# Adding two partial sums by accumulating transfers: an attention and MLP kernel on one Trainium2 core

## The chip, the core and the metric

The kernel runs on one core of one Trainium2 chip. A core has TensorE (matrix products, PE in the profile, with its weight loads as PEld), VectorE (DVE), ScalarE (ACT), GpSimd (POOL) and SyncE (SP). Each runs its own list of instructions in order, and they wait for each other by semaphores. Transfers (DMA) are issued by SP, ACT or POOL from their own lists, and a transfer issued by one of them is behind everything that stands earlier in that engine's list. The metric is the time of one execution on the device in microseconds. Three runs of the kernel before gave 1382.28, 1385.5 and 1387.74 us, so its median is 1385.5 us.

## The reference

The input x has 2048 tokens of 640 values. It is normalised once; xn goes through an attention block with 32 heads of 20 values, and through an MLP block with its own normalisation, 1536 hidden values and GELU. The output is x + attention + MLP.

```python
def _A_ref(x, wqkv, wo):
    ...
    scores = jnp.einsum("bhqd,bhkd->bhqk", q, k) * (Dh ** -0.5)
    p = _softmax(scores, axis=-1)
    o = jnp.einsum("bhqk,bhkd->bhqd", p, v)
    return (lambda x, *d: x.transpose(*d))(o, 0, 2, 1, 3).reshape(B, S, D) @ wo

def _B_ref(x, w1, b1, w2, b2):
    y = _layernorm(x, axis=-1)
    h = _gelu(jnp.einsum("bsd,df->bsf", y, w1) + b1)
    return jnp.einsum("bsf,fd->bsd", h, w2) + b2

x = A_x
xn = _layernorm(x, axis=-1)
return x + _A_ref(xn, A_wqkv, A_wo) + _B_ref(xn, B_w1, B_b1, B_w2, B_b2)
```

## The kernel before

The kernel has three stages. Up to about 290 us it normalises x, projects it to q, k and v, and splits the MLP's weights into two 16-bit halves. From there to about 1310 us it runs attention, with the MLP's products filled in between. After that comes the last part of the output projection.

**Attention.** Heads go in pairs `g`, tokens (queries) in two halves `hf` of 1024. The order of the 32 pieces is fixed in `ORDER`. A piece has two column halves `cc` of 512 queries, and 16 key blocks `kb` each. For every key block `scores` issues two products into the PSUM tile `s` (line 584) and one exponential on ScalarE into `p` (L586). For half of the key blocks (`SPLIT`) VectorE takes the lower half of p, `low` (L598), which `rest` records. `pv` issues the products with the values (L615) for a group of four key blocks, one group later than its scores. So TensorE needs a `low` about one group after VectorE could have made it.

Because of how the values lie in the array, each head's result comes in two partial sums. The products go to 32-row strips of the PSUM tile `o`; strips 0 and 1 belong to the first head of a pair, 2 and 3 to the second, and the two strips of one head have to be added. The same holds for the row sums, the softmax's denominators, which are a column of ones in the value matrix. `unload` writes the strips from the tile `ev` to scratch memory in HBM: `opart[p]` for the values and `lpart[p]` for the row sums, with p = 0 and 1 for the two partial sums.

**Finishing.** When a set of 2 or 3 pairs (`UNITS`, so 4 or 6 heads) is complete for one half of the tokens, `finish` loads the partial sums again, now as [heads x 20 rows, 512 tokens], and makes the normalised result. There are 12 finishes. Eleven have two chunks of 512 tokens (`w = 512`), the last one (`last`) has one of 1024. Per finish, the row sums are loaded to the tile `lt` (L675), added (L702), checked and inverted (L704 to L707), written to `linv` (L709) and read back spread over 20 rows per head as `rb` (L721). Per chunk, the two halves are loaded to the tile `oa` (L697), added (L725), multiplied by rb (L727), split into two 16-bit halves (L729, L731) and written to `oscr` (L732). The tile `oa` has one buffer, and the split result lies in the second half of it, so the loads of the second chunk wait for the write to oscr of the first.

**What sets the order.** The order of instructions is written out by hand: `finish` is a generator, and `tick` takes one step of each generator in `sides` after every two key blocks. Each `yield` in `finish` therefore moves what follows two key blocks later in the list of every engine. The loop takes MLP products from `fill` by a credit count, which does not depend on the generators in `sides` before the projection. MLP products go through one PSUM buffer (`psM`): VectorE must read it (L740 for the first layer, L757 for the second) before TensorE may start the next.

**Transfers.** Nearly all are issued by SP. GpSimd issues one kind in the attention stretch: `load_xb` loads 128 rows of x to the tile `xb` from SP (L808), and then GpSimd adds the bias b2 onto it by an accumulating transfer (L809). This occurs sixteen times.

Of the kernel before, what the change touches and what calls it, by code (L numbers as in the profile page):

```python
# [12 lines left out]
ALU = mybir.AluOpType  # L13
# [29 lines left out]
def mha_mlp_kernel(tc, x, wqkv, wo, w1, b1, w2, b2, out):  # L43
    nc = tc.nc
# [3 lines left out]
    with (  # L48
# [12 lines left out]
        opart = dram.tile([2, D, S], F32, name="opart")  # L61
        lpart = dram.tile([2, 2, H, S // 2], F32, name="lpart")
# [449 lines left out]
        with ExitStack() as scope:  # L512
# [127 lines left out]
            def dma(g, hf):  # L640

                return (nc.scalar if (g, hf) == ORDER[-1] else nc.sync).dma_start

            def unload(g, hf, ev):
                cols = slice(hf * 1024, (hf + 1) * 1024)
                for p in range(2):
                    dma(g, hf)(lpart[p, hf, 2 * g : 2 * g + 2, :].rearrange("a (c t) -> a c t", c=2),
                                      ev[PAD + DH + VW * p :: 64])
                    for a in range(2):
                        q0, r = 64 * a + PAD + VW * p, (2 * g + a) * DH  # L650
                        dma(g, hf)(opart[p, r : r + DH, cols].rearrange("d (c t) -> d c t", c=2),
                                          ev[q0 : q0 + DH])
                if g + 1 in ENDS:
                    fins.append(finish(g + 1 - UNITS[ENDS.index(g + 1)], g + 1, hf))
                    if len(fins) == 1:
                        sides.append(finishing())
# [9 lines left out]
            def finish(g0, g1, hf):  # L666
                nh, r0, r1 = 2 * (g1 - g0), 2 * g0 * DH, 2 * g1 * DH
                last = (g1 - 1, hf) == ORDER[-1]
                go = dma(g1 - 1, hf)
                w = 1024 if last else 512  # L670
                lt = m1.tile([P, 2, 64], F32, tag="lt", name="lt")
                n = checks.pop()
                yield
                for p in range(2):
                    go(lt[: nh * 16, p, :], lpart[p, hf, 2 * g0 : 2 * g1, :].rearrange("h (b t) -> (h b) t", t=64))  # L675
                for c0 in range(0, 1024, w):
                    cols = slice(hf * 1024 + c0, hf * 1024 + c0 + w)
                    if last:
                        o0, o1 = (ptp.tile([P, 2, 512], F32, tag="p", name="oa").rearrange("p c t -> p (c t)")
                                  for _ in range(2))  # L680
                        rb = o0

                        sel = [ptp.tile([P, 2, 512], F32, tag="p", name="sel").rearrange("p c t -> p (c t)")
                               for _ in range(2)]
                        for b0, t in zip((0, 8), sel):
                            nc.gpsimd.tensor_copy(
                                t[: nh * 16, : 8 * nh * DH].rearrange("p (b h d) -> p b h d", b=8, h=nh),
                                ident[: nh * 16, : nh * 16].rearrange("p (h b) -> p b h", b=16)[:, b0 : b0 + 8, :, None]
                                .to_broadcast([nh * 16, 8, nh, DH]))
                    else:  # L690
                        o = m1.tile([P, 2, 512], F32, tag="oa", name="oa")
                        o0, o1 = o[:, 0], o[:, 1]
                        rb = m1.tile([P, 512], F32, tag="rb", name="rb")
                    hl = o1.bitcast(F16).rearrange("p (s t) -> p s t", s=2)[: r1 - r0]
                    o0, o1, rb = o0[: r1 - r0], o1[: r1 - r0], rb[: r1 - r0]
                    for p, o in enumerate((o0, o1)):
                        go(o, opart[p, r0:r1, cols])  # L697
                    if c0 == 0:
                        for _ in range(W1 if last else 4):
                            yield  # L700
                        l = lt[: nh * 16]
                        nc.vector.tensor_add(l[:, 0], l[:, 0], l[:, 1])  # L702

                        nc.vector.tensor_scalar(l[:, 1], l[:, 0], LO, None, ALU.is_ge, ALU.min,  # L704
                                                accum_out=good[: nh * 16, n : n + 1])
                        nc.vector.tensor_scalar(l[:, 0], l[:, 0], 1e-30, None, ALU.max)
                        nc.vector.reciprocal(l[:, 1], l[:, 0])  # L707
                        if not last:
                            go(linv[hf, 2 * g0 : 2 * g1, :].rearrange("h (b t) -> (h b) t", t=64), l[:, 1])  # L709
                        for _ in range(4 if last else 1):  # L710
                            yield
                    if last:

                        rb = psS.tile([P, 2, 512], F32, tag="s", name="rb")[: nh * DH]
                        for b in range(16):
                            nc.tensor.matmul(rb[:, b // 8, b % 8 * 64 : b % 8 * 64 + 64],
                                             sel[b // 8][: nh * 16, b % 8 * nh * DH : (b % 8 + 1) * nh * DH],
                                             l[:, 1], start=True, stop=True)
                        rb = rb.rearrange("p c t -> p (c t)")
                    for h in range(0 if last else nh):  # L720
                        go(rb[h * DH : (h + 1) * DH],  # L721
                           linv[hf, 2 * g0 + h : 2 * g0 + h + 1, c0 : c0 + w].to_broadcast([DH, w]))
                    for _ in range(W2 if last else 4):
                        yield
                    nc.vector.tensor_add(o0, o0, o1)  # L725
                    yield
                    nc.vector.tensor_mul(o0, o0, rb)  # L727
                    yield
                    nc.vector.tensor_copy(hl[:, 0], o0)  # L729
                    yield  # L730
                    nc.vector.tensor_sub(hl[:, 1], o0, hl[:, 0])  # L731
                    go(oscr[:, r0:r1, cols].rearrange("s d t -> d s t"), hl)  # L732
                ready[hf] += 1
# [349 lines left out]
```

## Time and profile before

| | before |
|---|---|
| median of three runs | 1385.5 us |
| the profiled execution | 1385.2 us |
| its span, first to last instruction | 1383.5 us |
| TensorE busy | 1350.8 us |
| ScalarE busy | 1126.2 us |
| VectorE busy | 1061.7 us |
| GpSimd busy | 32.9 us |
| granted clock of TensorE | 0.997 |

The profile is of one execution. A row of a group or of the timeline names the engine, the line of the kernel, the operation, the tile written and the tiles read, the shape, and a count. "SPq" rows are issues of transfers by SP: their duration is that of the issue, not of the transfer. In square brackets stands how long the engine was idle before the instruction, and what ended this. In rows by tile the three durations are the least, the median and the greatest in ns, followed by the times at which the first and the last start. For transfers issued by GpSimd the profile also tells the time from issue to landing.

### The profile page before, as it was taken

What the parts mean: (1) busy time and instruction counts of PE and PEld (TensorE: products, weight loads), DVE (VectorE), ACT (ScalarE), POOL (GpSimd) and SP (SyncE); (2) the same over time, 40 slices, a digit from 0 to 9 for tenths busy, and PEclk for the clock granted to TensorE, in tenths of its full rate; (3) what the DMA queues carried; (4) which work ended last, traced back from release to release, by engine and by line L of the source; (5) the groups of instructions that cost most, each with busy time, mean ns of one, the idle gap of its engine ahead of it and who ended that gap; (6) DMA issues with size and microseconds to landing.
All of it is one profiled execution on the core that took longest, in us unless ns stands there. A gap on an engine that the chain in (4) does not pass through costs nothing.

```text
span 1383.5 us, 29113 instructions
## 1 busy us (share of the span) xinstructions
PE 1350.8 (98%) x11711; PEld 600.9 (43%) x11711; DVE 1061.7 (77%) x1425; ACT 1126.2 (81%) x1282; POOL 32.9 (2%) x75
## 2 busy tenths in 40 slices
PE   9999999999999999999999999999999999999998
PEld 6555555443333343433343333343334334333375
DVE  6648743899778977889887789877988897888642
ACT  5644323999999999999999999999999999999700
POOL 2000000000000000000000000000000000000000
PEclk9999999999999999999999999999999999999999
DMA  9853413012124231213221123212124322341375
GB/s 265 243 175 109 108 52 110 16 32 64 41 55 111 67 88 34 69 52 102 71 77 33 47 75 103 76 47 58 44 64 113 98 56 70 85 153 59 98 235 179
DMA packets 92320, 125.68 MB, mean 91 GB/s; under 512 B 16905, under 2 KB 58569, under 8 KB 92178
## 3 DMA queue, kind: packets, MB, share of 16 engines
q1 hardware_dynamic: 89218, 117.14, 28.3%
q0 software_dynamic: 2304, 5.24, 2.3%
q8 instruction: 94, 1.54, 0.5%
q10 hardware_dynamic: 656, 1.36, 0.3%
q14 instruction: 48, 0.39, 0.1%
HBM read 80.84 MB, written 42.86 MB: 89 GB/s over the span
## 4 chain that ended last, share of the span: by engine, by line
PE 59%; DVE 11%; ACT 5%; DMA 3%; issue 2%; SPq 1%; DVEq 0%; ACTq 0%
PE o L615 23%; PE s L584 14%; PE py L819 9%; PE pu L787 8%; DVE low L598 5%; PE z L896 5%; ACT p L586 4%; DMA oscr<-oa 1%; DVE u L740 1%; DMA oa<-opart 1%; DVE u L741 1%; DVE w L744 1%; DVE w L745 1%; DVE hT L752 1%; DVE u L750 1%
## 5 line engine op out<-in xcount | busy, mean ns | idle before, releaser
L586 ACT ACTIVATE p<-s 128x1024 f32<-128x1024 f32 x1024 | 973.6, 1042 | 52.4 <-PE s L584 46.2
L598 DVE TENSOR_TENSOR low<-p 128x1024 f16<-128x1024 f32 x512 | 608.8, 1219 | 165.0 <-ACT p L586 164.9
L615 PE MATMUL o<-p,vfull 128*32 128x512 bf16 (+1 forms) x4096 | 433.7, 494 | 0.0
L584 PE MATMUL s<-qs,ks 61*128 61x512 f16 x2048 | 317.7, 382 | 8.7 <-ACT p L586 7.2
L584 PEld LDWEIGHTS <-ks 61*128 61x128 f16 x2048 | 63.9, 94 | 296.4 <-issue 294.2
L787 PE MATMUL pu<-xm,w1t 128*128 128x256 f16 x1440 | 179.2, 274 | 4.1 <-DVE u L740 3.6
L819 PE MATMUL py<-w2t,hT 128*128 128x320 f16 x1152 | 178.6, 301 | 1.7 <-DVE xb L757 1.7
L787 PEld LDWEIGHTS <-w1t 128*128 128x128 f16 x1440 | 130.9, 98 | 71.2 <-issue 57.6
L819 PEld LDWEIGHTS <-hT 128*128 128x128 f16 x1152 | 102.5, 98 | 89.5 <-issue 55.2
L286 PE MATMUL qkp<-xnt,wv 128*128 128x512 f16 x600 | 132.3, 380 | 0.0
L615 PEld LDWEIGHTS <-vfull 128*32 128x32 f16 x3072 | 61.5, 95 | 146.2 <-issue 115.4
L615 PE MATMUL o<-low,vfull 128*32 128x512 f16 x1024 | 107.3, 379 | 6.6 <-DVE low L598 6.4
L300 ACT ACTIVATE qkhl<-qkp,qks 128x1024 f16<-128x1024 f32 (+1 forms) x24 | 23.3, 971 | 84.1 <-PE qkp L286 66.2
L286 PEld LDWEIGHTS <-wv 128*128 128x128 f16 x600 | 58.2, 98 | 67.8
L615 PEld LDWEIGHTS o<-p,vfull 128*32 128x32 f32 x2048 | 63.1, 109 | 50.6 <-issue 0.5
L349 PE MATMUL vp<-wv,xnt 128*128 128x320 f16 x480 | 66.6, 300 | 0.0
L896 PE MATMUL z<-w1t,ot 128*128 128x320 f16 x480 | 65.8, 300 | 0.0
L896 PEld LDWEIGHTS <-ot 128*128 128x128 f16 x480 | 46.7, 98 | 19.8 <-issue 1.7
L349 PEld LDWEIGHTS <-xnt 128*128 128x128 f16 x480 | 46.5, 98 | 18.2
L301 DVE SCALAR_TENSOR_TENSOR qkhl<-qkp,qks,qkhl 128x1024 f16<-128x1024 f32 (+1 forms) x24 | 26.5, 1104 | 34.3 <-ACT qkhl L300 34.3
L857 DVE SCALAR_TENSOR_TENSOR acc<-z,sc,acc 128x320 f32<-128x320 f32 x32 | 17.6, 550 | 45.1 <-PE z L896 42.9
L636 ACT ACTIVATE ev<-o 128x512 f32<-128x512 f32 x64 | 39.4, 615 | 3.3 <-PE o L615 3.3
(168 smaller groups left out, 685.7 us busy)
## 6 DMA issues: line engine op xcount, KB each, us to landing
qkscr<-qkhl SPq DMA_DIRECT2D x40, 256.0 KB
opart<-ev SPq DMA_DIRECT2D x124, 80.0 KB
ks<-qkscr SPq DMA_DIRECT2D x120, 80.0 KB
qs<-qkscr SPq DMA_DIRECT2D x192, 40.0 KB
oa<-opart SPq DMA_DIRECT2D x32, 240.0 KB
xt<-in_A_x_dram SPq DMA_DIRECT2D x16, 320.0 KB
xscr<-xnt SPq DMA_DIRECT2D x4, 1280.0 KB
xm<-xscr SPq DMA_DIRECT2D x8, 640.0 KB
```

The costliest lines, as they stand in the source:

```text
L286: nc.tensor.matmul(ps[:, i, :], wv[:, k, q, a, mm * P : (mm + 1) * P], xnts[c][:, k, b, :], start=(k + n == 0), stop=(k == KD - 1 and n == 2))
L300: nc.scalar.activation(hl[:, 0, i0:i1], ps[:, i0:i1], AF.Copy, scale=a)
L301: nc.vector.scalar_tensor_tensor(hl[:, 1, i0:i1], ps[:, i0:i1], a, hl[:, 0, i0:i1], ALU.mult, ALU.subtract)
L349: nc.tensor.matmul(ps[:, hf, :320], xnts[c][:, k, a, j * P : (j + 1) * P], wv[:, k, 2, b, hf * 320 : (hf + 1) * 320], start=(n == 0), stop ...
L584: nc.tensor.matmul(ps[:, a, :], ks[64 * a : 64 * a + 61, kb * P : (kb + 1) * P], qs[64 * a : 64 * a + 61, cc * 512 : (cc + 1) * 512], star ...
L586: nc.scalar.activation(pt, ps, AF.Exp, scale=QS)
L598: nc.vector.tensor_sub(low, pt, upper(pt))
L615: nc.tensor.matmul(pv.o[32 * q : 32 * q + 32, :], src[:, v0 - PAD * (1 - q % 2) :][:, :32], t, start=q not in pv.begun, stop=last, skip_gr ...
L636: nc.scalar.activation(evs[g, hf][:, cc], pv.o, AF.Copy)
L787: nc.tensor.matmul(ps[:, i], w1v[:, k, (f + i) // 4, a, fo_ : fo_ + P], xnt[:, k, b, :], start=(n == 0), stop=(n == 3 * KD - 1))
L819: nc.tensor.matmul(ps[:, :320], hTs[mc][:, f, a, j * P : (j + 1) * P], w2v[:, f, b, hf * 320 : (hf + 1) * 320], start=(n == 0), stop=(n == ...
L896: nc.tensor.matmul(ps[:, :320], ot[:, k, a, j * P : (j + 1) * P], wov[:, k, b, h * 320 : (h + 1) * 320], start=(n == 0), stop=(n == 3 * KD ...
```

## The change

In every finish but the last, the second partial sum is no longer loaded beside the first. It is transferred onto it, by a transfer issued by GpSimd that adds to what is there. This holds for the row sums (`lt`) and for both chunks of the values (`oa`). The two kinds of VectorE addition, and the `yield` behind the addition of the values, go away in these finishes; the last one is unchanged.

```diff
@@ finish @@
+                also = go if last else lambda o, i: nc.gpsimd.dma_start(o, i, accum_op=ALU.add)
                 for p in range(2):
-                    go(lt[: nh * 16, p, :], lpart[p, hf, 2 * g0 : 2 * g1, :].rearrange("h (b t) -> (h b) t", t=64))
+                    (go, also)[p](lt[: nh * 16, p * last, :],
+                                  lpart[p, hf, 2 * g0 : 2 * g1, :].rearrange("h (b t) -> (h b) t", t=64))
...
-                    for p, o in enumerate((o0, o1)):
-                        go(o, opart[p, r0:r1, cols])
+                    go(o0, opart[0, r0:r1, cols])
+                    also(o1 if last else o0, opart[1, r0:r1, cols])
                     if c0 == 0:
                         for _ in range(W1 if last else 4):
                             yield
                         l = lt[: nh * 16]
-                        nc.vector.tensor_add(l[:, 0], l[:, 0], l[:, 1])
+                        if last:
+                            nc.vector.tensor_add(l[:, 0], l[:, 0], l[:, 1])
...
                     for _ in range(W2 if last else 4):
                         yield
-                    nc.vector.tensor_add(o0, o0, o1)
-                    yield
+                    if last:
+                        nc.vector.tensor_add(o0, o0, o1)
+                        yield
                     nc.vector.tensor_mul(o0, o0, rb)
```

TensorE's list of instructions is the same in both kernels. In the lists of SP, VectorE and GpSimd, what follows a removed `yield` stands one step of the generator earlier.

## Prediction

> **What bounds the kernel now.** I read the page first (busy time, slices, chain), then the waits of TensorE in the attention stretch, then the rows of the two adds, then the timeline around single finishes.
>
> ```profile
> span 1383.5 us, 29113 instructions
> PE 1350.8 (98%) x11711; PEld 600.9 (43%) x11711; DVE 1061.7 (77%) x1425; ACT 1126.2 (81%) x1282; POOL 32.9 (2%) x75
> PE   9999999999999999999999999999999999999998
> DVE  6648743899778977889887789877988897888642
> q1 hardware_dynamic: 89218, 117.14, 28.3%
> q0 software_dynamic: 2304, 5.24, 2.3%
> ```
>
> TensorE is busy in all forty slices; VectorE has about a fifth of its time free in the middle. So work taken from VectorE is not time taken from the kernel. It counts only where TensorE waits for VectorE. The waits of TensorE between 290 and 1310 us are these:
>
> ```profile
> PE s L584 <- ACT p L586: 5.5, 20, 0.5
> PE o L615 <- DVE low L598: 5.4, 9, 1.5
> PE pu L787 <- DVE u L740: 3.6, 4, 2.0
> PE py L819 <- DVE xb L757: 1.7, 2, 1.3
> ```
>
> Columns: total us, times, longest. TensorE waits for VectorE 5.4 + 3.6 + 1.7 = 10.7 us in all. That is the most that any relief of VectorE in this stretch can return, 0.8% of the time, and only a part of it lies near a finish.
>
> **What the change removes.** The adds, and the transfers that feed them, by tile:
>
> ```profile
> L702 DVE TENSOR_TENSOR lt<-lt x12: 203/211/216, 417.4 to 1319.6; 96x64 f32<-96x64 f32 x8, 64x64 f32<-64x64 f32 x4
> L725 DVE TENSOR_TENSOR oa<-oa x23: 676/684/1209, 426.2 to 1330.3; 120x512 f32<-120x512 f32 x16, 80x512 f32<-80x512 f32 x6, 80x1024 f32<-80x1024 f32 x1
> L697 SPq DMA_DIRECT2D oa<-opart x44: 308/398/1439, 411.4 to 1276.5; - x44
> L809 POOL DMA_DIRECT2D xb<-in_B_b_dram x16: 854/867/1054, 318.0 to 1284.6; - x16
> ```
>
> Eleven of the twelve finishes change, each with one row-sum add and two value adds (a chunk of 512 tokens each). VectorE loses 11 x 0.21 + 22 x 0.69 = 17.5 us of work. SP loses 11 + 22 issues of about 0.4 us, some 13 us; SP is not a bound, and what stands behind these issues (stack loads for the next pair of heads) starts that much sooner: nothing. GpSimd's queue gains 33 issues of 0.87 us, 29 us spread over 900 us. The order of TensorE's instructions stays the same, so the change acts through waits alone.
>
> **What the change adds: a serial pair of transfers.** Before, both halves of a sum were loaded side by side. Now the second may only be issued once the first has landed, on GpSimd's queue, and the product with the reciprocals (L727, now the first VectorE step of a chunk) waits for it. The trace has such a pair already, x and then b2 added onto it:
>
> ```profile
> 509.84 0.36 SPq L808 DMA_DIRECT2D xb<-in_A_x_dram  x1
> 513.15 0.87 POOL L809 DMA_DIRECT2D xb<-in_B_b_dram  x1 [77.40 <-DMA xb<-in_A_x_dram]
> DMA to landing us min/median/max: 4.1/4.4/8.9
> ```
>
> From the load's issue to the accumulate's issue 513.15 - 509.84 = 3.3 us; from there to landing 4.1 at least, 4.4 in the middle. I take 4.2, as this place has little other traffic: 7.5 us for 320 KB. The chunk has 240 KB. By the queue rows, 5.24 MB of software transfers take 2.3% of 1383.5 us, so 80 KB less saves 0.50 us, and 117.14 MB of hardware transfers take 28.3%, so 80 KB less saves 0.27. Estimate: 6.7 us from the load's issue until the product may start, 6.0 for the three finishes of four heads (160 KB). Ends: 6.0 and 7.5.
>
> [...]
>
> **The row sums: nothing.** In the first finish:
>
> ```profile
> 410.53 0.78 SPq L675 DMA_DIRECT2D lt<-lpart  x2
> 417.39 0.21 DVE L702 TENSOR_TENSOR lt<-lt 96x64 f32<-96x64 f32 x1
> ```
>
> The add came 6.9 us after the load's issue. A pair of 24 KB each needs 7.5 less the data of nearly 300 KB (1.9 + 1.0), about 4.6 us. Two microseconds of cover remain; with none of the data term it would be 7.5, and the reciprocal would wait 0.6 us. What stands behind it on VectorE is the next low, on SP the write of linv.
>
> **The first chunk: nothing.** Its product comes 9 ticks after the load (the add at 426.2 by the row above, the load at 411.4), 15 us against 6.7 + 0.87 behind the row sums on GpSimd's queue.
>
> **The second chunk: here it costs.** Its buffer is freed by the write of the first chunk to oscr, so its load cannot be early, and its first VectorE step comes four ticks after that. Four cases, the load, the add, the low behind it and TensorE's use of that low:
>
> ```profile
> 482.59 1.41 SPq L697 DMA_DIRECT2D oa<-opart  x2
> 486.91 0.69 DVE L725 TENSOR_TENSOR oa<-oa 120x512 f32<-120x512 f32 x1 [1.22 <-DMA oa<-opart]
> 487.52 1.22 DVE L598 TENSOR_TENSOR low<-p 128x1024 f16<-128x1024 f32 x1
> 490.54 0.39 PE L615 MATMUL o<-low,vfull 128*32 128x512 f16 x4
> 493.38 1.22 DVE L598 TENSOR_TENSOR low<-p 128x1024 f16<-128x1024 f32 x1
> 494.45 0.60 PE L615 MATMUL o<-low,vfull 128*32 128x512 f16 x4
> 680.27 0.78 SPq L697 DMA_DIRECT2D oa<-opart  x2
> 685.46 0.69 DVE L725 TENSOR_TENSOR oa<-oa 120x512 f32<-120x512 f32 x1
> 686.06 1.22 DVE L598 TENSOR_TENSOR low<-p 128x1024 f16<-128x1024 f32 x1
> 688.38 0.39 PE L615 MATMUL o<-low,vfull 128*32 128x512 f16 x4
> 1139.91 0.77 SPq L697 DMA_DIRECT2D oa<-opart  x2
> 1143.63 0.69 DVE L725 TENSOR_TENSOR oa<-oa 80x512 f32<-80x512 f32 x1
> 1144.24 1.21 DVE L598 TENSOR_TENSOR low<-p 128x1024 f16<-128x1024 f32 x1
> 1147.50 0.39 PE L615 MATMUL o<-low,vfull 128*32 128x512 f16 x4
> 1202.62 0.77 SPq L697 DMA_DIRECT2D oa<-opart  x2
> 1210.01 0.68 DVE L725 TENSOR_TENSOR oa<-oa 80x512 f32<-80x512 f32 x1
> ```
>
> VectorE comes to the chunk 3.1 us after the load (486.91 less its 1.22 of waiting), 5.2, 3.7 and 7.4; the product takes the add's place in the order. So it will wait 6.7 - 3.1 = 3.6, 1.5, 6.0 - 3.7 = 2.3 and 0 us. In the first case 1.2 was waited before, so the low behind it is 2.4 late; it had 490.54 - 488.74 = 1.8 to spare. The low at 493.38 has nothing to spare (TensorE's 0.60 instead of 0.39 is its waiting), and reaches it 2.4 - 0.69 = 1.7 late, since the add is gone from its front: TensorE loses 1.7. In the second 1.5 against 688.38 - 687.28 = 1.1 spare: 0.4. In the third 2.3 against 2.05: 0.25. In the fourth 0. The mean of the four is 0.6 us; eleven finishes, 6 us. With ready at 6.0 the four lose 1.0, 0, 0, 0 (about 3 us in all); with 7.5 for all they lose 2.5, 1.2, 1.75 and 0.1 (about 15). Nothing hides a lost TensorE microsecond, since TensorE has no free slices.
>
> **What is gained.** In the first finish VectorE waited at the second chunk's add and then ran late, until TensorE waited for it:
>
> ```profile
> 435.58 0.79 SPq L697 DMA_DIRECT2D oa<-opart  x2
> 442.96 0.69 DVE L725 TENSOR_TENSOR oa<-oa 120x512 f32<-120x512 f32 x1 [0.47 <-DMA rb<-linv]
> 454.08 1.47 PE L787 MATMUL pu<-xm,w1t 128*128 128x256 f16 x12 [1.99 <-DVE u L740]
> ```
>
> Here VectorE comes 442.96 - 0.47 - 435.58 = 6.9 us after the load, late enough for the product, and what follows it is 0.7 us earlier. I count 3 of the 10.7 us as returned over all finishes, with 0 and 10.7 as ends.
>
> **Queues.** GpSimd is in order. A pair's second half standing in wait holds up the b2 transfer behind it by a few us at most; the tile xb is next read by VectorE when the 36 products of the next py are done, which are spread over many groups. SP waits for the last step of a chunk before it writes oscr; a product 2 us late holds the stack loads behind it by 2 us, which are wanted a whole stack (16 key blocks twice, over 30 us) later. The last finish keeps its adds, and the tail behind 1310 us is untouched.
>
> **Sum.** 1385.2 (the profiled execution) + 6 - 3 = 1388. It stood 0.3 us under the median of 1385.5.
>
> **Rivals.**
> 1. Relief wins, faster: the second half lands before VectorE comes to it. It needs ready at about 4.5 us, the middle of 3.1 to 7.4. The load of 320 KB alone takes 3.3 of the 6.7, which speaks against it. Then nothing is lost and 3 to 10.7 us return: 1375 to 1382.
> 2. Contention, clearly slower: the six loads of rb follow the chunk's load at once on SP, and run beside the accumulate. One b2 transfer ran just beside such loads:
>
> ```profile
> 434.89 0.85 POOL L809 DMA_DIRECT2D xb<-in_B_b_dram  x1 [51.45 <-DMA xb<-in_A_x_dram]
> DMA to landing us min/median/max: 6.7/6.7/6.7
> ```
>
> The mechanism is the landing at 6.7 instead of 4.2, ready at 9.2; the four cases then lose 4.2, 2.9, 3.4 and 1.8, 34 us in eleven, 1416. It passes +0.5% from about 7.3 us on (between the 6 us loss at 6.7 and 15 at 7.5). Against it: by the time the accumulate moves data, four to five us after the load, rb is nearly through; before, the whole pair of loads ran with it.
> [...]
>
> **How the numbers follow.** Forecast as summed 0.55, relief 0.12, contention 0.23 (mostly its beginning, a landing about 1 us late, 1394 to 1400), held issue 0.10. Range 1380 to 1400: below it lies half of rival 1, above it the strong form of rival 2. This kernel's measurement tells about 0.5%, 6.9 us, from no change: faster means under 1378.6, slower over 1392.4. Rival 1 gives 0.08 faster; rival 2 with the upper end of the forecast and of rival 3 gives 0.32 slower; 0.60 remain.
>
> **What would show it.** VectorE busy falls by some 17 us. L727 now has idle time before it, put to the transfer into oa, 1 to 3 us in most second chunks and none in first chunks; the row-sum step has none. Landing of the accumulates into oa is 3.5 to 4 us after issue. TensorE's waits for low and u grow by 2 to 6 us in all. I am wrong if landing exceeds 5 us, if first chunks wait too, or if TensorE's waits for VectorE fall below 7 us.

## The result, and the profile after

| | before | after |
|---|---|---|
| median | 1385.12 us (six runs) | 1400.62 us (six runs, 1398.21 to 1403.46) |
| ratio, 95% interval | 1 | 1.0106 [1.0095, 1.0117] |
| span of the profiled execution | 1383.5 us | 1396.4 us |
| VectorE's wait ahead of its steps on `oa` | 2.8 us | 31.9 us |
| TensorE's waits for VectorE, 290 to 1310 us (after: to 1330) | 10.7 us | 21.7 us |

The changed kernel is about 1.1% slower, some 15 us. Its profiled execution, 1398.2 us, is the fastest of its six runs. The lines of its page that answer to those of before:

```profile
span 1396.4 us, 29119 instructions
PE 1352.4 (97%) x11711; PEld 601.4 (43%) x11711; DVE 1047.0 (75%) x1392; ACT 1125.7 (81%) x1282; POOL 61.6 (4%) x108
PE   9999999999998899999999999999999999999998
DVE  6658743898777877888887778877978897788632
q1 hardware_dynamic: 85346, 111.98, 26.6%
q0 software_dynamic: 6320, 10.41, 4.6%
```

VectorE does 14.7 us less, GpSimd 28.7 us more, and TensorE has two slices that are no longer full. Next the waits between 290 and 1330 us of the changed kernel, of TensorE and then of VectorE (total us, times, longest):

```profile
PE o L615 <- DVE low L598: 9.2, 13, 1.7
PE s L584 <- ACT p L586: 5.4, 19, 0.5
PE pu L791 <- DVE u L744: 4.4, 5, 3.1
PE pu L791 <- DVE xb L761: 3.7, 2, 2.7
PE py L823 <- DVE u L744: 3.1, 3, 1.7
PE py L823 <- DVE xb L761: 1.3, 1, 1.3
```

```profile
DVE oa L731 <- DMA opart<-ev: 14.5, 4, 5.0
DVE oa L731 <- DMA oa<-opart: 13.8, 6, 4.3
DVE oa L731 <- DMA qs<-qkscr: 3.5, 1, 3.5
```

L731 is now the line of the product. All eleven waits in this second fence stand before a second chunk, 14.5 + 13.8 + 3.5 = 31.8 us, 2.9 on average (the 31.9 of the table has 0.1 of the last finish in it). Where another transfer than the one into `oa` is named, it is only the last event that the profile saw; the product reads nothing of `ev` or `qkscr`. First chunks do not wait. TensorE's waits for `low` grew from 5.4 to 9.2 us, those for `u` from 3.6 to 7.5, and those for `xb` from 1.7 to 5.0: 11.0 us more. `xb` is late because VectorE, held at the product, came late to it.

The accumulating transfers themselves, by tile, first those into `oa`, then those into `lt`:

```profile
L674 POOL DMA_DIRECT2D oa<-opart x22: 810/850/1098, 414.4 to 1289.4; - x22
DMA to landing us min/median/max: 3.2/4.2/5.3
```

```profile
L674 POOL DMA_DIRECT2D lt<-lpart x11: 833/837/865, 412.8 to 1260.1; - x11
DMA to landing us min/median/max: 2.2/3.7/4.1
```

In the eleven second chunks the accumulate is issued 3.0 to 4.8 us after the load, 3.6 on average, and lands 4.2 us after that on average; the product runs 6.5 to 9.6 us after the load's issue, 7.9 on average. The first finish, by the issues of SP and GpSimd, VectorE and TensorE (in brackets the idle time before):

```profile
434.89 0.34 SPq L698 DMA_DIRECT2D oa<-opart  x1
438.71 0.87 POOL L674 DMA_DIRECT2D oa<-opart  x1 [3.09 <-DMA oa<-opart]
443.12 0.69 DVE L731 TENSOR_TENSOR oa<-oa,rb 120x512 f32<-120x512 f32 x1 [5.04 <-DMA opart<-ev]
443.72 1.22 DVE L598 TENSOR_TENSOR low<-p 128x1024 f16<-128x1024 f32 x1
444.86 0.68 DVE L744 TENSOR_TENSOR u<-pu,r2f 128x512 f32<-128x512 f32 x1
445.60 3.69 PE L791 MATMUL pu<-xm,w1t 128*128 128x256 f16 x18 [3.12 <-DVE u L744]
```

VectorE comes to the product at 443.12 - 5.04 = 438.08, 3.2 us after the load, and the pair is ready 8.2 us after it. Behind the product stand a `low` and then the `u` of the MLP, which frees the PSUM buffer that TensorE wants: TensorE stands still for 3.12 us.

### The profile page after: what moved, and what is told of

Same layout as the page of the kernel before. It is cut to its first block, busy times and chain, and to the rows that moved or that the text cites. A ratio compares the mean times of both kernels' runs of the same rounds, so it can differ in the third digit from the quotient of the medians.

```text
span 1396.4 us, 29119 instructions
## 1 busy us (share of the span) xinstructions
PE 1352.4 (97%) x11711; PEld 601.4 (43%) x11711; DVE 1047.0 (75%) x1392; ACT 1125.7 (81%) x1282; POOL 61.6 (4%) x108
## 4 chain that ended last, share of the span: by engine, by line
PE 57%; DVE 12%; ACT 6%; DMA 3%; issue 3%; SPq 1%; ACTq 0%; DVEq 0%; POOLq 0%
PE o L615 22%; PE s L584 14%; PE py L823 9%; PE pu L791 8%; DVE low L598 6%; ACT p L586 5%; PE z L900 5%; DMA oa<-opart 2%; DVE u L744 1%; DVE u L745 1%; DMA opart<-ev 1%; DVE w L748 1%; DVE hT L756 1%; DVE w L749 1%; DVE u L754 1%
```

## The experiments

The first theory, "wait": the loss is the second chunk's wait for the serial pair, passed on by VectorE to TensorE, and the row sums and first chunks cost nothing. Its rivals: "place" (the removed `yield` moves the finish's steps to other neighbours, and that alone costs time) and "transfers" (the accumulates disturb other work wherever they are). All kernels compute the full result. In the diffs, e4 and e7 are against the kernel before, the others against the changed one. A ratio is always to the kernel before on the same chip, with its 95% interval in brackets. TensorE's waits for VectorE are counted from 290 us on.

**e1: the second chunk in halves again, added by VectorE; the rest accumulated.**

```diff
-                    also(o1 if last else o0, opart[1, r0:r1, cols])
+                    if last or c0:
+                        go(o1, opart[1, r0:r1, cols])
+                    else:
+                        also(o0, opart[1, r0:r1, cols])
...
-                    if last:
+                    if last or c0:
                         nc.vector.tensor_add(o0, o0, o1)
                         yield
```

> The row sums and the first chunk stay accumulating transfers; the second chunk of the eleven finishes is loaded in two halves and added by VectorE again. Wait theory (the product of the second chunk waits for the serial pair, and nothing else costs): 1382 to 1387 us, no wait for oa over 1.5 us. Traffic theory (accumulating transfers as such disturb the rest): half of the 15 us stays, about 1393. Shift theory (steps stand one tick earlier and meet the MLP's steps worse): 1393 to 1400, since the first chunk's yield is still gone.

Measured: 1385.12 us, 0.9989 [0.9979, 0.9998]. VectorE's wait ahead of the steps on `oa` falls from 31.9 to 7.9 us, TensorE's waits for VectorE to 11.8. So 22 of the 33 accumulates, those into `lt` and into the first chunks, cost nothing, and "transfers" falls for them. The whole loss hangs on what was done to the second chunk.

**e2: only the second chunk accumulates.** Row sums and first chunk are loaded in halves and added, with the first chunk's `yield`.

```diff
...
-                    if last:
+                    if last or c0 == 0:
                         nc.vector.tensor_add(o0, o0, o1)
                         yield
```

> The opposite: only the second chunk is summed by an accumulating transfer; row sums and first chunk are as before the change. Wait theory: 1397 to 1402 us, the same 32 us of VectorE waiting before the second chunk's product, give or take a third. Traffic theory: about 1393. If row sums or first chunks were the cause: 1384 to 1387.

Measured: 1418.3 us, 1.0225 [1.0208, 1.0242]. That is twice the loss of the whole change, which "wait" in its simple form does not give. The product's waits add up to 46.2 us, and TensorE's waits for VectorE to 34.8:

```profile
PE o L615 <- DVE low L598: 31.1, 21, 4.3
```

The product starts a little later than in the changed kernel (7.2 to 10.6 us after the load, 8.4 on average, where it was 7.9), and VectorE comes sooner in several finishes: 1.5 us after the load in the worst one, where the wait is 7.6 us. And other work stands behind the product. One finish on VectorE, and TensorE just after it:

```profile
1115.99 0.69 DVE L733 TENSOR_TENSOR oa<-oa,rb 120x512 f32<-120x512 f32 x1 [6.91 <-DMA ks<-qkscr]
1116.60 0.68 DVE L756 SCALAR_TENSOR_TENSOR u<-w,u 128x512 f32<-128x512 f32 x1
1117.32 0.49 DVE L757 TENSOR_SCALAR hT<-u,sc 128x512 f16<-128x512 f32 x1
1117.84 0.75 DVE L758 SCALAR_TENSOR_TENSOR hT<-u,sc,hT 128x512 f16<-128x512 f32 x1
1118.51 1.22 DVE L598 TENSOR_TENSOR low<-p 128x1024 f16<-128x1024 f32 x1
```

```profile
1119.78 0.58 PE L615 MATMUL o<-low,vfull 128*32 128x512 f16 x1 [4.32 <-DVE low L598]
```

Three steps of the MLP, 1.9 us, stand between the late product and the `low` that TensorE waits for. In the changed kernel the same finish waits 0.5 us, and a `low` follows at once.

**e3: the changed kernel, product of the second chunk seven ticks after the load instead of four.**

```diff
-                    for _ in range(W2 if last else 4):
+                    for _ in range(W2 if last else 4 if c0 == 0 else 7):
                         yield
```

> The changed kernel with one number changed: seven ticks instead of four between the loads of the second chunk and its product. All accumulating transfers stay. Wait theory: the VectorE waits of 0.5 to 5 us before the product vanish (6 us more against pairs that take 6.5 to 9.6), and the time falls to 1381 to 1387 us. Traffic theory and shift theory: it stays at 1396 to 1402.

Measured: 1379.82 us, 0.9954 [0.9938, 0.9971]. The product now comes 9.1 to 13.1 us after the load and does not wait at all (0.07 us). TensorE's waits for VectorE are down to 6.9 us:

```profile
PE o L615 <- DVE low L598: 3.7, 6, 1.0
PE pu L791 <- DVE u L744: 1.9, 4, 1.0
PE py L823 <- DVE xb L761: 1.3, 1, 1.3
```

All transfers are as in the changed kernel, so neither they nor GpSimd's issues carry the loss by themselves. The wait does, or the place of the product, which has moved as well; e5 tells these two apart.

**e4: the kernel before without the `yield` behind the addition**, in the eleven finishes; both additions stay.

```diff
                     nc.vector.tensor_add(o0, o0, o1)
-                    yield
+                    if last:
+                        yield
```

> The kernel before with only the yield between add and product taken away in the eleven finishes; no accumulating transfer. Wait theory: 1383 to 1388 us. Shift theory: 1393 to 1400.

Measured: 1392.77 us, 1.0039 [1.0027, 1.0050]. No transfer is changed, and yet VectorE's wait before the steps on `oa` rises from 2.8 to 14.7 us and TensorE's waits for VectorE to 15.1. "Place" is a part of the matter of its own, since VectorE now comes to a plain pair of loads before it has landed. Of the 9 us between the two profiled spans up to 3.4 belong to TensorE's clock, which was at half for 6.8 us around the longest wait below (last section):

```profile
DVE oa L725 <- DMA oa<-opart: 9.5, 3, 4.7
PE pu L788 <- DVE u L741: 4.6, 4, 3.6
```

**e5 and e6: accumulate early.** Both chunks are loaded and accumulated at the start of the finish, into the two halves of `oa`, and the split result goes to the tile `rb`. e6 gives the second chunk six ticks as well.

```diff
-                        o = m1.tile([P, 2, 512], F32, tag="oa", name="oa")
-                        o0, o1 = o[:, 0], o[:, 1]
+                        if c0 == 0:
+                            both = m1.tile([P, 2, 512], F32, tag="oa", name="oa")
+                        o0 = both[:, c0 // w]
                         rb = m1.tile([P, 512], F32, tag="rb", name="rb")
+                        o1 = rb
...
+                    elif c0 == 0:
+                        for c in range(2):
+                            part = slice(hf * 1024 + c * w, hf * 1024 + (c + 1) * w)
+                            go(both[: r1 - r0, c], opart[0, r0:r1, part])
+                            also(both[: r1 - r0, c], opart[1, r0:r1, part])
```

> Both chunks of a finish are loaded and accumulated at its start, into the two halves of the tile oa; the split result goes to the tile rb instead, so the second chunk's values no longer wait for the first chunk's write. Only its rb still does. Four ticks as in the changed kernel, all accumulating transfers stay. Wait theory: the product then waits for six plain loads instead of a serial pair, at most 1 to 2 us in some finishes: 1379 to 1387 us. Traffic theory: 1396 or more.

> The same with six ticks before the second chunk's product, so that rb has landed too. Wait theory: no waits of VectorE in the finishes, 1377 to 1381 us, as seven ticks gave with the late pair. If the place of the steps beside the MLP's steps matters more than waits, it can come out on either side of that by more than 3 us.

Measured: e5 1383.15 us, 0.9975 [0.9958, 0.9991]; e6 1384.08 us, 0.9972 [0.9947, 0.9996]. With the pair loaded some 25 to 35 us ahead of the second chunk's product the loss is gone although the product stands at the same four ticks: the wait made the loss, not the place alone. What is left in e5, 6.2 us before the steps on `oa`, is put to the loads of `rb`. Six ticks take that wait away (0.5 us in e6) and win nothing more.

**e7: the kernel before with seven ticks** (the diff of e3, made to before).

> The kernel before, with seven ticks instead of four before the second chunk's add; no accumulating transfer. It tells whether the gain of the changed kernel with seven ticks is VectorE's relief or just the later place. Relief: 1382 to 1386 (only the 2.8 us of waits for oa go away). Later place alone: 1378 to 1381.

Measured: 1382.06 us, 0.9965 [0.9948, 0.9983]. The later place alone, without any accumulating transfer, gives about what e3 gave.

**e8: the changed kernel with five ticks.**

> The changed kernel with five ticks before the second chunk's product, one more. Wait theory: each of the eleven waits shrinks by a tick of 2.1 us, from 31.8 us in all to about 13, and the time goes some 60 percent of the way to that of seven ticks: 1386 to 1391 us. Shift theory (the first chunk's missing yield): 1395 to 1401.

Measured: 1386.24 us, 1.0001 [0.9980, 1.0021]. With four, five and seven ticks the product's waits in second chunks are 31.8, 13.2 and 0 us, TensorE's waits for VectorE 21.7, 13.3 and 6.9, the ratios 1.0106, 1.0001 and 0.9954. The time follows the wait step by step.

**e9: the changed kernel with the `yield` of the first chunk put back, and nothing else.** It separates whether e2 was so slow by its additional work or by the place of its steps.

```diff
                     if last:
                         nc.vector.tensor_add(o0, o0, o1)
+                    if last or c0 == 0:
                         yield
```

> The changed kernel with the yield put back in the first chunk alone; no add, all accumulating transfers stay. Everything from the first chunk's product on stands one tick later against the MLP's steps, as in the kernel with only the second chunk accumulated, which took 1418 us. Place theory (how long VectorE waits and how much of it reaches TensorE depends on which steps of the MLP stand beside the second chunk): 1408 to 1420 us. Work theory (that kernel was slower than the changed one because VectorE still had 11 + 11 more adds): 1396 to 1402.

Measured: 1423.53 us, 1.0248 [1.0214, 1.0281]. One `yield`, no work, and by the two ratios 1.4%, about 20 us, more than the changed kernel. The waits (45.7 us) and what stands behind them are those of e2, where the same finish again has the three MLP steps behind the product. So e2's excess comes with the place of its steps and not with its additions.

**e10 and e11: e3 and e7 again, side by side on one chip**, to ask whether the accumulating transfers are worth anything once the wait is gone.

> The changed kernel with seven ticks in the second chunk again, beside the kernel before with seven ticks on the same chip. Relief of VectorE counts: at least 0.3 percent (4 us) faster than the other. Relief counts for nothing: within 0.15 percent (2 us) of it.

> The kernel before with seven ticks, for the comparison with the run above. Relief counts: 1383 to 1386 us. Relief counts for nothing: 1379 to 1383 us.

Measured: e10 1378.97 us, 0.9959 [0.9944, 0.9975]; e11 1380.32 us, 0.9958 [0.9945, 0.9971]. Both beat both kernels by a small amount, and they cannot be told apart: what VectorE no longer adds is worth nothing that can be measured here.

## Why the prediction was right or wrong, point by point

The time, 1400.6 us, lies 12.6 us above the forecast of 1388, at the upper end of its range (0.6 us over 1400); not the likeliest case came, no measurable change, but the one with the chance of 0.32, slower. The mechanism was the forecast's own, with its sizes too small. That the end of the range lies so near is luck: it was set for transfers that land late, and they did not. By the steps:

- **What relief can return.** Held in the end: e10 against e11 gives nothing for it. VectorE's busy time fell by 14.7 us and not by 17.5, since neighbouring steps overlap a little: in the rows shown of before, the 0.69 us addition at 486.91 was followed by the next step 0.61 later.
- **Row sums and first chunk: nothing.** Right. The row-sum step waits 0.4 us in all, first chunks do not wait, and e1 shows no cost.
- **GpSimd's queue and the held issue.** No run shows the held issue that has 0.10 of the chances and a part in the 0.32: the 33 accumulating issues took 0.81 to 1.10 us, most of them 0.85, like the sixteen of before (0.85 to 1.05).
- **The pair ready at 6.7 us, 6.0 for four heads.** This is the first mis-sized term. The two parts that were read from the pair of x and b2, 3.3 us and 4.2, measured 3.6 and 4.2. The pair needed 8.1 us on average with six heads and 7.2 with four, 7.9 over all eleven, more than the upper end of 7.5. Most of what is missing is the 0.8 us (and 1.5 for four heads) that was taken off for fewer bytes, since on average neither part came out shorter than in the larger pair; the rest is that the first part was longer. Its slots were sized well in the mean: four cases at 3.1 to 7.4, mean 4.9; measured 2.7 to 8.0, mean 5.0. Singly they moved: the case at 482 us waited 3.50 (3.6 foretold), the one at 680 waited 2.29 (1.5), at 1140 it was 2.22 (2.3), and the one at 1203, foretold at 0, waited 3.79. The waits came to 31.8 us where 1.85 in each of eleven would be 20.
- **The loss of 6 us at TensorE.** The second mis-sized term. TensorE's waits for VectorE grew by 11.0 us, close to the 15 that the prediction worked out for a pair at 7.5 us. A third of this fell on `u` and a third on `xb`; the working in the prediction had followed `low` alone. Two of its sums are slightly off: with the 3 us taken off as returned, its points (6 us lost at 6.7, 15 at 7.5) pass +0.5% at a pair of about 7.1 us and not 7.3, and at 6.0 the third case still loses its 0.25.
- **The 3 us returned.** The step that failed outright. The first finish was to come 0.7 us earlier, since VectorE would arrive 6.9 us after the load. It arrived after 3.2 us, waited 5.04, and TensorE lost 3.12. The prediction moved the product into the place of the addition, but not the second chunk's steps as a whole against the MLP's steps, which the first chunk's missing `yield` does; e4 shows that taking the `yield` out alone costs 0.4%, and e9 that a shift the other way costs far more, in both with a part of TensorE's clock (its mean was 0.995 in e4 and 0.987 in e9, against 0.997 before; last section).
- **Only waits count.** Not quite: TensorE's granted clock fell once between 290 and 1330 us, to 0.50 for 3.4 us (last section), which by estimate costs up to 1.7 us. 11.0 + 1.7 = 12.7 of the 12.9 us between the two profiled spans.
- **Rival 2, contention.** The time was near its beginning, but not its mechanism: the landing into `oa` was 4.2 us at the median, as taken, and 5.3 at most, far from 6.7. The product waited for a pair of the assumed kind in slots that were too short.
- **Its signs.** Idle time before the product came in all eleven second chunks and in no first one, as foretold, but up to 5.0 us of it and not 3. VectorE's relief (14.7 us for 17) was below its figure; TensorE's waits for `low` and `u` (7.7 us more for 2 to 6) and the median landing (4.2 for 3.5 to 4) were above theirs. One sign of being wrong appeared: 2 of the 22 landings into `oa` passed 5 us, by 0.3 at most.

## What to carry to other kernels

A load followed by an accumulating transfer is a serial pair, here 7.9 us until the result may be read where two loads side by side hardly made VectorE wait (in e1 such waits ended 3.9 to 4.2 us after the issue, once 7.1). So it belongs far ahead of its reader, or the reader later, and relieving an engine with spare time was worth nothing here. Work that an in-order engine waits with is charged to whatever stands behind it (in the first finish 3.12 us of TensorE's time behind a product that waited 5.04): when a step or a `yield` is removed, look up which steps become the new neighbours, since moving them by one place cost up to 1.4% here (e9 against the changed kernel), more than the 1.1% of the change itself. TensorE's clock can add to a wait: the gap of 3.12 us in the changed kernel came with 3.4 us at half clock, the one of 4.32 us in e2 with 6.8, by estimate up to 1.7 and 3.4 us more. Before adopting such a change, give the kernel before the same freedom of place: with it, the kernels were equal.

## What the runs showed of the hardware that was not expected

In some standstills of TensorE its granted clock fell to half (0.50 and 0.51 in the rows below), and stayed there for 3.4 or 6.8 us. Stretches of the changed kernel around the first finish (columns: window and its length, then busy us of PE, PEld, DVE, ACT and POOL with counts, the granted clock, the DMA share and GB/s), and of e2 around the finish shown above:

```profile
440.00:445.40 5.40, 2.47 (x26) 0.67 (x25) 2.29 (x3) 4.43 (x5) 0.00 (x0) 1.00 0.55 129
445.40:448.90 3.50, 3.31 (x16) 2.36 (x16) 3.43 (x6) 0.00 (x0) 0.00 (x0) 0.51 0.00 0
448.90:455.00 6.10, 6.10 (x64) 2.48 (x65) 5.77 (x8) 5.29 (x7) 0.00 (x0) 1.00 0.57 154
```

```profile
1111.00:1117.80 6.80, 4.46 (x44) 1.52 (x45) 1.78 (x3) 4.66 (x5) 0.00 (x0) 1.00 0.60 134
1117.80:1124.70 6.90, 4.04 (x18) 0.78 (x18) 6.23 (x8) 2.10 (x3) 0.00 (x0) 0.51 0.16 40
1124.70:1131.00 6.30, 6.30 (x66) 2.94 (x68) 4.95 (x5) 5.59 (x7) 0.00 (x0) 1.00 0.25 88
```

A mean of 0.51 over 3.50 us is half clock for 3.50 x 0.49 / 0.5 = 3.4 us; 0.51 over 6.90 us is 6.8 us. TensorE's standstill was 3.12 us in the first (442.5 to 445.6) and 4.32 in the second (to 1119.8), and the clock fell before it ended. A gap of 2.68 us in the changed kernel, at 488 us, brought no drop. In e2 there were five drops: 6.8 us each at gaps of 3.48, 3.71, 4.32 and 2.62 us (the last with one of 0.89 close by), and 3.4 us at two shorter gaps close together, 1.37 and 1.09. An estimate from these lengths: at half clock a microsecond costs at most half of itself, where TensorE is busy; that is up to (4 x 6.83 + 3.41) / 2 = 15.4 us in e2; with its 24.1 us of additional waits for VectorE that makes 39.5, and its span is 38.5 longer than that of before. By this, waits that reached TensorE were charged about half as much again in e2, and e2 and e9, whose profiled executions both have a mean granted clock of 0.987 (0.997 before), cost more than their waits. The kernel before has no such drop in the attention stretch, nor has e3; e4 has one of 6.8 us at a gap of 3.55, e5 one of 3.4.

The length of a gap alone does not tell whether a drop came: 2.68 us in the changed kernel brought none, and two gaps of 1.37 and 1.09 in e2 brought one. In each trace the drops begin a whole number of 3.413 us apart: in the kernel before at 15.92 and 237.79 us, 65 such steps, and in the changed kernel at 15.33, 237.19 and 445.41 us, 65 and 61 steps; each of these five lasts 3.413 us. So the gaps are counted here by stretches of this length, laid out from a drop's beginning. Three of the changed kernel: the one that ends with the drop, the next one, and the one with the larger part of the gap of 2.68 us:

```profile
442.00:445.41 3.41, 0.47 (x4) 0.10 (x1) 2.29 (x3) 2.43 (x3) 0.00 (x0) 1.00 0.40 123
445.41:448.82 3.41, 3.23 (x16) 2.29 (x16) 3.34 (x6) 0.00 (x0) 0.00 (x0) 0.50 0.00 0
486.37:489.79 3.42, 1.60 (x15) 1.44 (x15) 3.42 (x6) 1.09 (x2) 0.00 (x0) 1.00 0.41 126
```

TensorE stood still for 3.41 - 0.47 = 2.94 us of the first and 3.42 - 1.60 = 1.82 of the third. Counted like this over all thirteen traces between 300 and 1330 us, the ten stretches at full clock with 2.2 us of standstill or more were all followed by half clock, of nineteen with 1.4 to 2.0 us two were (1.78 in e2, 1.43 in e5), and of those with less none. In the first stretch at half clock TensorE stood for at most 0.22 us in the four cases where it lasted for one (3.41 - 3.23 = 0.18 in the rows above), and for 0.84 us or more in the eight where it lasted for two.

Still open: why two of the nineteen stretches with less standstill were followed by half clock, and why the other five runs of the changed kernel took up to 5 us longer than the profiled one. Further drops of the clock would explain most of it: the mean granted clock of those runs was 0.993 to 0.995 against 0.996, which is about 3 to 8 us more at half clock and up to 4 us of time; but those runs have no trace.
